# Split weights of the first MLP at another offset within their SBUF slots

## The chip, the cores and the metric

The kernel runs on one core of one Trainium2 chip. The metric is the device time of one execution in microseconds. Three runs of the kernel before gave 1238.68, 1238.93 and 1238.98 us, median 1238.93.

## What is computed

Three float32 stages follow one another; the weights of both MLPs come as 64-bit floats:

```python
# attention: 4 batches x 12 heads, 448 rows, head size 64
q_n, k_n = rmsnorm(q, g_q), rmsnorm(k, g_k)
x = softmax(q_n @ k_n.T / sqrt(64)) @ v            # -> 4 x 448 x 768
# first MLP, with layer norm and residual
xn = layernorm(x) * g_ln
y = x + relu(xn @ w_ch1) @ w_ch2                   # 768 -> 3072 -> 768
# gated MLP
h = relu(y @ w_in); u, v = h[..., :512], h[..., 512:]
v_s = einsum('ts,bsd->btd', w_spatial, layernorm(v)) + b_spatial
out = (u * v_s) @ w_out
```

## The kernel before, in words

Attention goes first, then the first MLP, then the gated MLP, one after the other on TensorE, with the seams overlapped. In the two MLPs every float32 operand is split in two float32r parts, a high part (a rounded copy) and a low part (the rest), and each product is three matmuls: high by high, high by low, low by high (the table `THREE`). The first number of a pair picks the part of the stationary operand, the second that of the moving one.

The first MLP works in units of 128 hidden columns, 24 units in all. For a unit u and a batch b, `h_pe` (L703) makes the hidden block: 6 slices of the 768 inputs by 3 products are 18 matmuls, with a 128x128 block of w_ch1 as the stationary operand and the normalized input `xn` (128 x 448) as the moving one. `h_act` and `h_dve` (L713, L718) take it out of PSUM as the split tile `h`. `o_pe` (L726) multiplies it by w_ch2: 6 output blocks by 3 products, again 18 matmuls with a stationary 128x128 block of weights. So there are 24 x 4 x 36 = 3456 matmuls, each 128x128 by 128x448, and all of them load their stationary operand from a `ws` tile.

A `ws` tile holds one unit's block of one weight matrix in both parts, 2 x 768 float32r values in each partition. It is made in `plan_parts`: ScalarE copies the converted weights `wc` into the high part (`hi`, through the helper at L101), GpSimd subtracts to get the low part (`lo`, L178). The conversion from 64-bit numbers (L91 to L95) stands ahead of it on ScalarE and VectorE. There are five slots for `ws` tiles: two in the pool `w0s`, which during attention also holds the normalized keys and queries (`kq`), and three in the pool `w1s`, which opens with the first MLP. The order of all instructions on every engine is written out by a planner (`arrange`) from estimated times and due numbers; it knows nothing of addresses.

In the gated MLP the same scheme of three products is used, with other tiles: `gv` (L797; moving `winv` 128x512, stationary the split `ys`, 112 columns), `gu` (L860; moving `ys` 128x448, stationary `winu`, 128 columns), `gs` (L881; moving `wsp_s` 112x448, stationary `gvs`, 128 columns), `gp` (L928; moving `wout` 128x384, stationary `gg`, 128 columns). `ys` lies in the buffer that held the `xn` of batch 0.

Where the tiles lie, from the built program: the first byte in the partition, and in brackets what is left after division by 256. All steps inside these tiles from slice to slice are multiples of 256 bytes, except in `ys` as a stationary operand, where the four column blocks c of 112 stand 448 bytes apart.

| tile | before | after |
|---|---|---|
| `ws`, pool `w0s` | 174048, 180192 (224) | 173728, 180128 (160) |
| `ws`, pool `w1s` | 103392, 109536, 115680 (224) | 102304, 108704, 115104 (160) |
| `kq`, in the slots of `w0s` | 174048, 180192 (224) | 173536, 179936 (224) |
| `xn`, batches 0 to 3 | 17120, 38624, 121824, 143328 (224) | 17120, 38624, 121312, 142816 (224) |
| `h` | 92640, 96224, 99808 (224) | 91360, 94944, 98528 (224) |
| `wc` | 89568, 170976 (224) | 88288, 170464 (224) |
| `ys` moving (`gu`) | 17120 (224) | the same |
| `ys` stationary (`gv`), c = 0, 1, 2, 3 | (224), (160), (96), (32) | the same |
| `winu`, stationary (`gu`) | 103072 (160) | the same |
| `winv`, moving (`gv`) | 60128 (224) | the same |
| `wsp_s` moving, `gvs` stationary (`gs`) | 88736 (160), 38624 (224) | the same |
| `wout` moving, `gg` stationary (`gp`) | 159200 (224), 200672 (224) | the same |

Of the kernel before, what the change touches and what calls it, by code (L numbers as in the profile page):

```python
# [10 lines left out]
F32R = mybir.dt.float32r  # L11
# [23 lines left out]
def f32(ap):  # L35
    return ap.bitcast(F32)
# [3 lines left out]
def attention_mlp_gated(ctx, tc, q, k, v, g_q, g_k, g_ln, w1, w2, w_in, w_sp, b_sp, w_out, out):  # L40
    nc = tc.nc
    B, H, S, D = q.shape
    DM, FF = w1.shape
    DG = w_out.shape[0]
    P = 128
# [54 lines left out]
    def act_copy(d, s):  # L100
        nc.scalar.activation(d, s, AF.Copy)  # L101
# [6 lines left out]
    wpools = {"raw": [], "c": [], "s": []}  # L108
    wsp, converted, pieces = {}, {}, []
# [56 lines left out]
    def plan_parts(i, n, since=()):  # L166
        kind, src, u = pieces[i]
        pl, c = converted[i], f"wc{i}"

        def hi():  # L170
            m = n_split[0] % 5
            n_split[0] += 1
            t = wsp[kind, u] = wpools["s"][int(m > 1)].tile([P, 2, DM], F32R, tag="ws", name=f"ws{i}")
            act_copy(t[:, 0], pl["c"])

        def lo():
            t = wsp[kind, u]
            nc.gpsimd.tensor_tensor(t[:, 1], pl["c"], f32(t[:, 0]), op=ALU.subtract)  # L178

        if kind == "gate":  # L180
            dma(n, src.shape[1] / 2, lambda: nc.sync.dma_start(u, pl["c"]), r=[c])
        else:
            op(n, "ACT", 0.73, hi, r=[c, *since], w=[f"{kind}_{u}"], new="ws")
            op(n, "POOL", 1.76, lo, r=[c], w=[f"{kind}_{u}"])
# [23 lines left out]
    def op(n, eng, us, fn, r=(), w=(), new=None, mode=None):  # L208

        ops.append((n, eng, us, fn, tuple(r), tuple(w), new, mode))  # L210

    def dma(n, kb, fn, **kw):

        op(n, "SP", max(0.6, kb / 360), fn, **kw)
# [757 lines left out]
    with tc.manual_schedule():  # L972
# [148 lines left out]
        n, i = 49, len(conv_at) + 3  # L1121
# [155 lines left out]
```

## Time and profile before

| | |
|---|---|
| median of three runs | 1238.93 us |
| profiled execution: its own time | 1238.33 us |
| profiled execution: span | 1236.3 us |
| TensorE busy | 1208.0 us, 98% of the span |
| VectorE, ScalarE, GpSimd busy | 796.3, 451.1, 325.3 us |
| matmuls of L703 and L726 | 1728 and 1728, 365.7 and 366.1 us busy |

The busy time of a group is the time in which at least one of its instructions ran; matmuls overlap, so that a single one is recorded with 365 ns while the next one starts well before that is over. What a matmul costs in a dense stretch is read from starts: the timeline merges like instructions into one row with the start of the first and their count, so the start of the next row less this start, divided by the count, is the cost of each.

### The profile page before, as it was taken

The numbers are of one execution on the slowest core, as the hardware profiler recorded it, in microseconds if no ns is written. First come the engines' busy times: TensorE is split into PE (matmuls) and PEld (weight loads), VectorE is DVE, ScalarE is ACT, GpSimd is POOL, SyncE is SP. The second block draws the span as 40 slices with busy tenths as digits, with TensorE's granted clock in tenths as the row PEclk, the third lists the DMA queues.
The fourth block names the chain that finished last, engine by engine and source line by source line (L and its number), as shares of the span: only waits on it lengthen the run. The fifth ranks groups of instructions, "written<-read, shape, count | busy, mean of one in ns | idle before, by whom it ended". The sixth has DMA issues, their size and how long they took to land.

```text
span 1236.3 us, 16695 instructions
## 1 busy us (share of the span) xinstructions
PE 1208.0 (98%) x6528; PEld 1021.6 (83%) x6528; DVE 796.3 (64%) x1436; ACT 451.1 (36%) x910; POOL 325.3 (26%) x266
## 2 busy tenths in 40 slices
PE   3999999999999999999999999999999999999998
PEld 1655656656999999999999999999999988889898
DVE  6889998976988656474747484755535577342240
ACT  2888888987432212131312121221202122123112
POOL 5764767524121102020202111010201115312120
PEclk9999999999999999999999999999999999999999
DMA  4213122111214232231313141502100053111103
GB/s 104 76 53 76 53 54 75 49 49 34 77 69 137 69 102 71 83 110 44 111 43 119 50 155 44 153 26 77 52 26 26 26 211 109 40 45 51 39 1 90
DMA packets 50861, 89.00 MB, mean 72 GB/s; under 512 B 3952, under 2 KB 39152, under 8 KB 50016
## 3 DMA queue, kind: packets, MB, share of 16 engines
q1 hardware_dynamic: 50352, 83.82, 22.1%
q10 hardware_dynamic: 432, 4.13, 0.8%
q8 instruction: 51, 0.84, 0.3%
q14 instruction: 26, 0.21, 0.1%
HBM read 73.58 MB, written 14.35 MB: 71 GB/s over the span
## 4 chain that ended last, share of the span: by engine, by line
PE 87%; DVE 9%; DMA 2%; POOL 1%; ACT 1%; issue 0%; SPq 0%; DVEq 0%
PE ph L703 28%; PE pm L726 28%; PE s L473 5%; PE gp L928 5%; PE po L523 4%; PE t L506 4%; PE gv L797 4%; PE gu L860 3%; PE gs L881 3%; DVE nmx L479 2%; DMA y_dram<-y 1%; PE pk L450 1%; DMA wout_r<-wout_dram 1%; DVE rt L80 1%; PE pq L450 1%; PE pxT L578 1%
## 5 line engine op out<-in xcount | busy, mean ns | idle before, releaser
L726 PE MATMUL pm<-h,ws 128*128 128x448 f32 x1728 | 366.1, 365 | 0.0
L703 PE MATMUL ph<-xn,ws 128*128 128x448 f32 x1728 | 365.7, 365 | 0.0
L726 PEld LDWEIGHTS pm<-h,ws 128*128 128x128 f32 x1728 | 324.3, 188 | 26.4 <-issue 0.7
L703 PEld LDWEIGHTS ph<-xn,ws 128*128 128x128 f32 x1728 | 324.4, 188 | 25.8 <-DVE y L734 0.2
L178 POOL TENSOR_TENSOR ws<-wc,ws 128x768 fp32r<-128x768 f32 x48 | 95.9, 1997 | 583.7 <-ACT ws L101 571.5
L734 DVE TENSOR_TENSOR y<-pm,y 128x448 f32<-128x448 f32 x318 | 176.1, 613 | 78.7 <-PE pm L726 78.7
L713 ACT ACTIVATE h<-ph 128x448 fp32r<-128x448 f32 x96 | 51.8, 540 | 276.5 <-PE ph L703 269.2
L718 DVE SCALAR_TENSOR_TENSOR h<-ph,h 128x448 fp32r<-128x448 f32 x96 | 59.6, 621 | 131.8 <-ACT h L713 130.2
L483 ACT ACTIVATE P<-s,nmx 112x448 f32<-112x448 f32 x192 | 119.2, 635 | 30.4 <-DVE nmx L479 30.1
L479 DVE TENSOR_REDUCE nmx<-s 112x2 f32<-112x896 f32 x96 | 101.1, 1080 | 18.7 <-PE s L473 18.2
L91 ACT ACTIVATE wc<-wr 128x768 f32<-128x768 f32 (+1 forms) x64 | 55.1, 862 | 136.6 <-POOL ws L178 45.2
L473 PE MATMUL s<-kT,qT 64*112 64x448 f32 x384 | 88.2, 580 | 0.6 <-ACT qT L459 0.6
L506 PE MATMUL t<-ident,P 112*112 112x112 f32 x768 | 85.4, 260 | 1.6 <-ACT P L483 1.1
L101 ACT ACTIVATE ws<-wc 128x768 fp32r<-128x768 f32 x48 | 40.6, 846 | 115.5 <-PE ph L703 99.2
L506 PEld LDWEIGHTS t<-ident,P 112*112 112x112 f32 x768 | 76.0, 133 | 4.8 <-ACT P L483 3.8
L523 PE MATMUL po<-PT,vr 112*64 112x448 f32 x384 | 77.5, 545 | 0.0
L95 DVE SCALAR_TENSOR_TENSOR wc<-wr,wc 128x768 uint32<-128x768 uint32 (+1 forms) x64 | 69.1, 1079 | 1.1
L94 DVE SCALAR_TENSOR_TENSOR wc<-wr,wc 128x768 int32<-128x768 int32 (+1 forms) x64 | 67.6, 1056 | 1.6
L92 DVE TENSOR_SCALAR wc<-wc 128x768 f32<-128x768 f32 (+1 forms) x64 | 37.4, 584 | 47.0 <-ACT wc L91 46.9
L797 PE MATMUL gv<-winv,ys 128*112 128x512 f32 x288 | 67.3, 393 | 0.0
L473 PEld LDWEIGHTS s<-kT,qT 64*112 64x112 f32 x384 | 31.4, 178 | 41.6 <-issue 23.4
L523 PEld LDWEIGHTS po<-PT,vr 112*64 112x64 f32 x384 | 25.4, 136 | 48.5 <-issue 38.4
(167 smaller groups left out, 1270.1 us busy)
## 6 DMA issues: line engine op xcount, KB each, us to landing
wr<-in_moe_w_ch_dram SPq DMA_DIRECT2D x48, 768.0 KB, 4.4
wr<-in_moe_w_in_dram SPq DMA_DIRECT2D x12, 512.0 KB, 3.8
vr<-in_v_dram SPq DMA_DIRECT2D x24, 224.0 KB, 2.7
kr<-in_k_dram SPq DMA_DIRECT2D x11, 448.0 KB, 3.9
qr<-in_q_dram SPq DMA_DIRECT2D x11, 448.0 KB, 4.8
y_dram<-y ACTq DMA_DIRECT2D x3, 1344.0 KB, 9.0
yl<-y_dram SPq DMA_DIRECT2D x3, 1344.0 KB, 6.2
win_dram<-wc SPq DMA_DIRECT2D x12, 256.0 KB, 5.1
```

The source lines that it names most:

```text
L94: lambda: v.scalar_tensor_tensor(ci, hi, -0x40000000, ci, op0=ALU.bitwise_and, op1=ALU.bitwise_or),
L95: lambda: v.scalar_tensor_tensor(cu, lo.bitcast(U32), 29, cu, op0=ALU.logical_shift_right, op1=ALU.bitwise_or),
L178: nc.gpsimd.tensor_tensor(t[:, 1], pl["c"], f32(t[:, 0]), op=ALU.subtract)
L473: nc.tensor.matmul(p[:CP, j, :S], pr["qT"][rows, c * CP : (c + 1) * CP], pr["kT"][rows], start=True, stop=True)
L479: nc.vector.tensor_reduce(t, pr["s", c][:CP, :, :S], axis=AX.X, op=ALU.max, negate=True)
L483: nc.scalar.activation(t, pr["s", c][:CP, j, :S], AF.Exp, bias=pr["m", c][:, j : j + 1], scale=1.0, accum_out=pr["sum"][:, j, c : c + 1],)
L506: nc.tensor.transpose(p[:CP, e, c * CP : (c + 1) * CP], pr["P", j, c][:, kc * CP : (kc + 1) * CP], ident[:CP, :CP])
L523: nc.tensor.matmul(pr["po"][j * D : (j + 1) * D, :S], raw["v", i][:, j, kc, :], pr["PT", kc // 2, j][:, kc % 2], start=(kc == 0), stop=(kc ...
L703: nc.tensor.matmul(hid[u, b][0][:, :S], s1[:, a, kk, :], xn[b][:, c, kk, :], start=(kk == 0 and m == 0), stop=(kk == NK - 1 and m == 2),)
L726: nc.tensor.matmul(po[:, :S], s2[:, a, m * P : (m + 1) * P], hs[:, c, :], start=(first and e == 0), stop=(last and e == 2),)
L734: nc.vector.tensor_tensor(y[b][:, m, :], po[:, :S], y[b][:, m, :], op=ALU.add)
L797: nc.tensor.matmul(pv[:CP, :], ys[b][:, a, kk, c * CP : (c + 1) * CP], W["v", kk][:, e], start=(kk == 0 and m == 0), stop=(kk == NK - 1 an ...
```

## The change

The slot of a `ws` tile is 64 float32 values (256 bytes) longer, and the split weights begin 48 values (192 bytes) into it. Every stationary address of L703 and L726, and every write of L101 and L178 to `ws`, moves with them; nothing else reads these tiles. The pools that are allocated behind these slots move down by 512 or 1280 bytes, whole multiples of 256. Instructions, their operands' shapes and their order on every engine are the same as before.

```diff
@@ -170,7 +170,9 @@
         def hi():
             m = n_split[0] % 5
             n_split[0] += 1
-            t = wsp[kind, u] = wpools["s"][int(m > 1)].tile([P, 2, DM], F32R, tag="ws", name=f"ws{i}")
+            t = wsp[kind, u] = wpools["s"][int(m > 1)].tile([P, 2 * DM + 64], F32R, tag="ws", name=f"ws{i}")[
+                :, 48 : 48 + 2 * DM
+            ].rearrange("p (a f) -> p a f", a=2)
             act_copy(t[:, 0], pl["c"])
```

## Rows read from the trace of the kernel before

**Rows 1.** Page: busy time by engine, TensorE and clock over 40 slices.

```profile
PE 1208.0 (98%) x6528; PEld 1021.6 (83%) x6528; DVE 796.3 (64%) x1436; ACT 451.1 (36%) x910; POOL 325.3 (26%) x266
...
PE   3999999999999999999999999999999999999998
...
PEclk9999999999999999999999999999999999999999
```

**Rows 2.** Page: the chain that ended last, by engine and by line.

```profile
PE 87%; DVE 9%; DMA 2%; POOL 1%; ACT 1%; issue 0%; SPq 0%; DVEq 0%
PE ph L703 28%; PE pm L726 28%; PE s L473 5%; PE gp L928 5%; PE po L523 4%; PE t L506 4%; PE gv L797 4%; PE gu L860 3%; PE gs L881 3%; DVE nmx L479 2%; DMA y_dram<-y 1%; PE pk L450 1%; DMA wout_r<-wout_dram 1%; DVE rt L80 1%; PE pq L450 1%; PE pxT L578 1%
```

**Rows 3.** Waits of TensorE over the span: total us, times, longest.

```profile
PE pk L450 <- DVE kq L412: 13.4, 1, 13.4
PE pk L450 <- POOL kq L412: 6.4, 1, 6.4
PE t L506 <- ACT P L483: 1.1, 4, 0.6
PE psp L1197 <- DVE wsp_s L1203: 0.8, 1, 0.8
PE gs L881 <- POOL gvs L838: 0.7, 1, 0.7
```

**Rows 4.** Windows: busy us (instructions) of each engine, clock, DMA.

```profile
core 0: us, PE busy (x) PEld busy (x) DVE busy (x) ACT busy (x) POOL busy (x), PEclk, DMA share, GB/s
...
328.00:1014.00 686.00, 686.00 (x3387) 634.54 (x3386) 428.17 (x673) 147.33 (x221) 96.96 (x50) 1.00 0.24 79
...
1038.00:1236.00 198.00, 193.57 (x977) 174.99 (x975) 71.06 (x139) 45.64 (x88) 39.13 (x28) 1.00 0.14 42
```

**Rows 5.** Timeline of TensorE, 600 to 632 us, first MLP: start, us, what.

```profile
602.41 3.81 PE L703 MATMUL ph<-xn,ws 128*128 128x448 f32 x18
606.06 3.81 PE L726 MATMUL pm<-h,ws 128*128 128x448 f32 x18
...
631.60 0.57 PE L703 MATMUL ph<-xn,ws 128*128 128x448 f32 x2
```

**Rows 6.** Timeline of TensorE, 1103 to 1164 us, gated MLP.

```profile
1109.11 14.56 PE L860 MATMUL gu<-ys,winu 128*128 128x448 f32 x72
1123.51 29.31 PE L928 MATMUL gp<-wout,gg 128*128 128x384 f32 x168
1152.66 9.87 PE L881 MATMUL gs<-wsp_s,gvs 112*128 112x448 f32 x48
1162.36 1.80 PE L797 MATMUL gv<-winv,ys 128*112 128x512 f32 x7
```

**Rows 7.** The same, 1172 to 1216 us.

```profile
1178.91 14.56 PE L860 MATMUL gu<-ys,winu 128*128 128x448 f32 x72
1193.31 9.87 PE L881 MATMUL gs<-wsp_s,gvs 112*128 112x448 f32 x48
```

**Rows 8.** Timeline of weight loads, batch 2, blocks c = 0 to 3 (four windows).

```profile
1092.36 4.08 PEld L797 LDWEIGHTS gv<-winv,ys 128*112 128x112 f32 x18
1096.49 4.08 PEld L797 LDWEIGHTS gv<-winv,ys 128*112 128x112 f32 x18
1100.63 4.11 PEld L797 LDWEIGHTS gv<-winv,ys 128*112 128x112 f32 x18
1104.81 4.03 PEld L797 LDWEIGHTS gv<-winv,ys 128*112 128x112 f32 x18
```

**Rows 9.** The same for batch 1, block c = 3.

```profile
1064.06 4.11 PEld L797 LDWEIGHTS gv<-winv,ys 128*112 128x112 f32 x18
```

**Rows 10.** Timeline, 312 to 330 us: the first units.

```profile
311.84 0.77 PE L726 MATMUL pm<-h,ws 128*128 128x448 f32 x3
312.45 0.93 PE L578 MATMUL pxT<-ident,x 112*128 112x112 f32 x8
313.33 7.57 PE L703 MATMUL ph<-xn,ws 128*128 128x448 f32 x36
```

**Rows 11.** Timeline of all engines, 354 to 364 us: the third unit's weights.

```profile
356.71 0.85 ACT L101 ACTIVATE ws<-wc 128x768 fp32r<-128x768 f32 x1 [1.55 <-DVE wc L95]
...
357.63 2.22 POOL L178 TENSOR_TENSOR ws<-wc,ws 128x768 fp32r<-128x768 f32 x1 [30.93 <-ACT ws L101]
...
361.44 2.62 PEld L703 LDWEIGHTS ph<-xn,ws 128*128 128x128 f32 x13
```

**Rows 12.** Groups by line and form, 328 to 1014 us: makers of `ws`, a load.

```profile
L178 POOL TENSOR_TENSOR ws<-wc,ws 128x768 fp32r<-128x768 f32 x44 | 88.3, 2008 | 537.4 <-ACT ws L101 525.1 <-issue 12.3
...
L101 ACT ACTIVATE ws<-wc 128x768 fp32r<-128x768 f32 x44 | 37.2, 845 | 111.9 <-PE ph L703 99.2 <-PE pm L726 6.2 <-DVE wc L95 5.9
...
L797 PEld LDWEIGHTS gv<-winv,ys 128*112 128x112 f32 x30 | 5.2, 174 | 1.6
```

## Prediction

> **What bounds the kernel now.** I read the page first, then the waits of TensorE, the windows by stage, and last the timeline of TensorE alone, since the question is what one matmul costs. The page shows TensorE busy for 98% of the span, with the clock granted in full in all 40 slices [rows 1]. In the chain that ended last TensorE has 87%, and the two lines of the first MLP, L703 and L726, have 28% each: 56% of the span hangs on the 3456 matmuls whose stationary operand is the tile that moves [rows 2]. The waits of TensorE are two long ones for `kq` at the start and then a microsecond here and there; no line of the first MLP stands among the longest [rows 3]. Between 328 and 1014 us TensorE is busy in all of the 686.0 us, while VectorE has 428.2, ScalarE 147.3 and GpSimd 97.0 [rows 4]. There the end is set by nothing but the pace of the matmuls, and any change of that pace reaches the end in full.
>
> A busy TensorE is not one at its best pace, so the pace itself has to be looked at. From 602.41 to 631.60 us there are eight groups of 18 matmuls: 29.19 us over 144 is 202.7 ns each [rows 5]. At 2.4 GHz, the upper level of the clock, 448 columns are 186.7 ns, so 16.0 ns come on top. In the gated MLP the line `gu` has the same shape, 128x128 by 128x448, and the same order of three products, and its moving operand lies in the very buffer that holds `xn` of batch 0 here. It takes 1123.51 - 1109.11 = 14.40 us for 72 matmuls, 200.0 ns each [rows 6], and the same 14.40 us one batch later [rows 7]: 13.3 ns on top of its columns. `gp` with 384 columns takes 29.15 us for 168, 173.5 ns, which is 160.0 + 13.5 [rows 6]. The fourth column block of `gv` in batch 2, with 512 columns, has 17 intervals and one load of 174 ns in 4.03 us: 226.8 ns, or 213.3 + 13.5 [rows 8, 12]. So three shapes agree on a floor of columns plus 13.3 to 13.5 ns, and the matmuls of the first MLP stand 2.7 ns above it.
>
> What raises a matmul above the floor is seen best inside `gv`, where the moving operand, the shape and the order are the same in the four blocks of a batch, and only the stationary operand begins elsewhere: at 224, 160, 96 and 32 bytes past a multiple of 256. The starts give 4.13 us, 4.14 us and 4.18 us for 18 in the first three, 229.4, 230.0 and 232.2 ns, against 226.8 in the fourth [rows 8]. The place of the stationary operand is thus worth up to 5.4 ns per matmul. `gs`, with its moving operand at 160 and its stationary one at 224, has 9.70 us for 48, 202.1 ns [rows 6], also above the 200.0 of its column count.
>
> **The change part by part.** It adds no instruction, no wait and no transfer, and moves none past another on any queue, SP's and GpSimd's among them. What it moves is the stationary address of 3456 matmuls, from 224 to 160 past a multiple of 256, while their moving operands stay at 224. That pair, 160 and 224, at 448 columns and 128 stationary columns, is the pair of `gu`. So the row that stands nearest to the changed matmul is 200.0 ns, and I take it.
>
> The sum: the first 18 of L703 and the first 18 of L726 lie among the last attention work, before the row at 313.33 us [rows 10], and I leave them out; 3456 - 36 = 3420 matmuls gain 202.7 - 200.0 = 2.7 ns each, unrounded 2.71, together 9.3 us. The unknown price of the pair is bounded from both sides by the rows of `gv`: best, at the floor, as in the fourth block, -9.3 us; worst, 5.4 ns above it, as in the third, (5.4 - 2.7) x 3420 = +9.2 us. I take the lower end because `gu` shares shape, order and moving buffer with the changed lines, and no `gv` row does.
>
> One rule of the Trainium skill speaks against this. First the rows: the same moving buffer and the same shape run at 202.7 ns with one stationary tile and at 200.0 ns with another [rows 5, 6], and four column blocks of one stationary tile differ by up to 5.4 ns [rows 8]. The Trainium skill, "TensorE: Matmul & The Clock Gate", Part 2 (step by step, on LDWEIGHTS), says that TensorE has two independent read ports, so that loading the next weights takes nothing from the running matmul; by that the place of the weights would not matter and the time would stay at 1238.9 us. The rows of this trace do not bear it out to the last nanosecond, which is where this change lives; so the rule keeps a chance as the first rival, no more.
>
> The writers of `ws` move too. The copy takes 845 ns on ScalarE and the subtraction 2008 ns on GpSimd [rows 12]; no row has either at the new offset, so their price is anything from a gain to a doubling. It is hidden: GpSimd is busy for 97.0 of 686.0 us [rows 4], and the tightest hand-over is the third unit's, whose low part is done at 357.63 + 2.22 = 359.85 us while its first load starts at 361.44, 1.59 us later [rows 11]. A faster TensorE comes there earlier by 2.7/202.7 of the 48.1 us since 313.33, 0.64 us; 0.95 us of cover is left. If the subtraction took more than 0.95 us longer, this one unit would wait for the difference, once, under 1.3 us even when it doubled. I take zero.
>
> With TensorE 1.3% faster in this stretch, VectorE's share goes from 428.2/686.0, 62%, to 63%, and the transfers, at a mean share of 0.24 [rows 4], have room; nothing is late next.
>
> The pools behind the slots move by whole multiples of 256, and the gated MLP's tiles do not move: zero for both, in time per instruction. One thing can flip there: the fourth block of `gv` ran at 226.8 ns in batch 2 and, with the same addresses, at (4.11 - 0.174)/17 = 231.5 ns in batch 1 [rows 8, 9]. So the pace also hangs on how a stretch is entered. Four such blocks x 18 x 4.7 ns are 0.34 us; two may flip either way, +-0.2 us.
>
> The sum against the profiled execution: its span is 1236.3 us and its own time 1238.33, so 2.0 us lie around the span; 1238.33 - 9.3 = 1229.0. That execution is 0.6 us under the median of the three runs, 1238.93, so on the scale of the median the forecast is 1238.93 - 9.3 = 1229.7 us.
>
> **The rivals.** The first: nothing happens, 1238.9 us. Either the 2.7 ns come from something other than the place of the weights (the PSUM buffers, or the distance of 3072 bytes between the two parts, which in `winu` is 2048), or the shift keeps whatever matters. For it: `gp` has both operands at 224 and stands at its floor, 173.5 ns [rows 6], so 224 with 224 is not bad at every column count. Against it: `gv` changes its pace with nothing but the column block [rows 8]. Chance 12%.
>
> The second ends on the other side: the new pair makes matmul and weight load meet more often, not less. In `gv` block 1, at 160 with 224 as after the change, is 230.0 ns, 0.6 ns slower than block 0 at 224 with 224 [rows 8]. If the order of `gv` holds, L703 and L726 go from 2.7 ns above the floor to about 2.7 x 3.2/2.6 = 3.3, which is +2.1 us, 1241.0; at the third block's 5.4 ns it is 1238.9 + 9.2 = 1248.1. It decides from a pace above 202.7 ns on. Against it stands that `gv` has 512 columns and 112 stationary ones, and `gu`, with the right numbers of both, is at the floor in each row that I have [rows 6, 7]. Chance 15%.
>
> The third: the floor is reached in part of the stretch alone. For it: the fourth block of `gv` has two paces at one address [rows 8, 9]; and of the five new slots only two (173728 and 108704) agree with `winu` in their rest after division by 512 too, the other three being 256 further. If two in five units gain, it is 0.4 x 9.3 = 3.7 us, 1235.2; if half the time is gained, 1234.3. Against it: the moving slices of 1792 bytes step by 256 from one to the next modulo 512, in `gu` and in L703 alike, so that either relation has occurred in `gu`, and its whole 72 still come out at 200.0 [rows 6]. Chance 9%.
>
> **How the numbers follow.** The forecast, near the floor throughout, has 64%, and its own range is 1228.8 to 1230.8: +-0.3 us for the spread of the runs, the flips in `gv`, up to 0.7 us for the third unit's cover. The range that holds the time 8 times in 10 starts at 1228.7 and goes up through the third rival and the first to 1239.5, which leaves out the second rival, 15%, and a little below. No change within 0.2% (2.5 us, about what a measurement of this kernel can tell from none) is 1236.5 to 1241.4: the first rival's 12%, and one part in three of the second, 5%, together 17%. Slower is the rest of the second, 10%. Faster is 64% + 9%, 73%.
>
> **What would show it.** In the changed kernel's timeline the groups of 18 should start 3.60 us apart in place of 3.65, in L703 and L726 alike, whatever the batch or the slot; `gu`, `gp`, `gs` and `gv` should keep their paces; the waits of TensorE should show no `ws`. If only the units of two slots quicken, the third rival was right; if the groups stand 3.65 us apart, the first; 3.66 or more, the second. The forecast fails at the step from `gu` to L703 if anything but the place of the weights sets their 2.7 ns.

## The result, and the profile after

Five runs of the changed kernel have the median 1229.24 us (1227.83 to 1229.59), five of the kernel before beside them 1238.93 us. The ratio is 0.9918 with a 95% interval of 0.9907 to 0.9930: 9.7 us less, and forecast were 9.3. The profiled execution took 1229.24 us with a span of 1227.5, 8.8 us less than the span before. All line numbers behind L174 are two higher in the changed kernel.

The page of the changed kernel, busy time and the chain by engine and line:

```profile
PE 1198.8 (98%) x6528; PEld 1020.5 (83%) x6528; DVE 794.9 (65%) x1436; ACT 451.3 (37%) x910; POOL 325.1 (26%) x266
...
PE 89%; DVE 7%; DMA 2%; ACT 1%; issue 0%; POOL 0%; SPq 0%; DVEq 0%
PE ph L705 28%; PE pm L728 28%; PE s L475 5%; PE gp L930 5%; PE gu L862 5%; PE gv L799 4%; PE po L525 4%; PE t L508 4%; PE gs L883 3%; DVE nmx L481 2%; DMA win_ru<-win_dram 1%; PE pk L452 1%; PE pq L452 1%; PE pxT L580 1%; DVE PT L518 1%; PE px L559 1%
```

Against [rows 1, 2] the number of instructions is the same and TensorE is busy for 9.2 us less, while the other engines keep their busy times within 1.5 us. In the chain L705 and L728 keep their 28% each, and TensorE has 89% in place of 87%. The reader should notice how little the page tells: a share of 98% stays 98% while the work inside it gets faster.

The pace, in the timeline of TensorE in the first MLP of the changed kernel:

```profile
603.22 3.76 PE L728 MATMUL pm<-h,ws 128*128 128x448 f32 x18
606.82 3.76 PE L705 MATMUL ph<-xn,ws 128*128 128x448 f32 x18
...
628.41 3.76 PE L705 MATMUL ph<-xn,ws 128*128 128x448 f32 x18
```

Seven groups of 18 take 628.41 - 603.22 = 25.19 us, 199.9 ns each, where [rows 5] had 202.7. The groups start 3.60 us apart. In the gated MLP of the changed kernel nothing moved:

```profile
1100.26 14.56 PE L862 MATMUL gu<-ys,winu 128*128 128x448 f32 x72
1114.66 29.31 PE L930 MATMUL gp<-wout,gg 128*128 128x384 f32 x168
1143.81 9.87 PE L883 MATMUL gs<-wsp_s,gvs 112*128 112x448 f32 x48
1153.52 2.72 PE L799 MATMUL gv<-winv,ys 128*112 128x512 f32 x11
```

`gu` takes 14.40 us for its 72, `gp` 29.15 for 168, `gs` 9.71 for 48, to 0.01 us what [rows 6] show.

The whole span can be cut at two starts, the first pair of hidden blocks in the dense stretch ([rows 10], 313.33 us) and the first `gv`. Timeline of TensorE, the kernel before:

```profile
1007.33 2.92 PE L797 MATMUL gv<-winv,ys 128*112 128x512 f32 x12
```

and the two places in the kernel after (two windows):

```profile
314.30 7.47 PE L705 MATMUL ph<-xn,ws 128*128 128x448 f32 x36
...
999.21 4.07 PE L799 MATMUL gv<-winv,ys 128*112 128x512 f32 x17
```

The stretch took 694.00 us before and takes 684.91 after: -9.09 us. The attention ahead of it ends 0.97 us later in this execution, the rest behind it is 0.68 us shorter (228.97 and 228.29); the sum is -8.80, the difference of the spans. The waits of TensorE in the kernel after show where most of the 0.97 comes from:

```profile
PE pk L452 <- DVE kq L414: 14.1, 1, 14.1
PE pk L452 <- POOL kq L414: 6.4, 1, 6.4
PE psp L1199 <- DVE g L815: 1.1, 1, 1.1
```

The wait for the first keys is 14.1 us in place of the 13.4 of [rows 3], 0.7 of the 0.97. The wait of `gs` for GpSimd, 0.7 us in [rows 3], is gone, while that of `psp` (small transposes in the gated MLP) is 1.1 us in place of 0.8: together 0.4 of the 0.68. These are seams outside the first MLP, and no `ws` stands among the longest waits.

The hand-over that was tightest, in the timeline of all engines of the kernel after:

```profile
358.10 2.23 POOL L180 TENSOR_TENSOR ws<-wc,ws 128x768 fp32r<-128x768 f32 x1 [30.37 <-ACT ws L101]
...
358.42 3.76 PE L728 MATMUL pm<-h,ws 128*128 128x448 f32 x18
...
361.82 3.58 PEld L705 LDWEIGHTS ph<-xn,ws 128*128 128x128 f32 x18
...
362.01 3.76 PE L705 MATMUL ph<-xn,ws 128*128 128x448 f32 x18
```

The subtraction takes 2.23 us, as before (2.22), and 1.49 us of cover are left of the 1.59 in [rows 11]. The prediction left only 0.95: counted from the start of the dense stretch, the load is 0.59 us earlier than before, but the subtraction is 0.50 us earlier too.

### The profile page after: what moved, and what is told of

It reads as the page before. It is cut to its first block, busy times and chain, and to the rows that moved or that the text cites. A ratio compares the mean times of both kernels' runs of the same rounds, so it can differ in the third digit from the quotient of the medians.

```text
span 1227.5 us, 16696 instructions
## 1 busy us (share of the span) xinstructions
PE 1198.8 (98%) x6528; PEld 1020.5 (83%) x6528; DVE 794.9 (65%) x1436; ACT 451.3 (37%) x910; POOL 325.1 (26%) x266
## 4 chain that ended last, share of the span: by engine, by line
PE 89%; DVE 7%; DMA 2%; ACT 1%; issue 0%; POOL 0%; SPq 0%; DVEq 0%
PE ph L705 28%; PE pm L728 28%; PE s L475 5%; PE gp L930 5%; PE gu L862 5%; PE gv L799 4%; PE po L525 4%; PE t L508 4%; PE gs L883 3%; DVE nmx L481 2%; DMA win_ru<-win_dram 1%; PE pk L452 1%; PE pq L452 1%; PE pxT L580 1%; DVE PT L518 1%; PE px L559 1%
## 5 line engine op out<-in xcount | busy, mean ns | idle before, releaser
L728 PE MATMUL pm<-h,ws 128*128 128x448 f32 x1728 | 361.6, 362 | 0.0
L705 PE MATMUL ph<-xn,ws 128*128 128x448 f32 x1728 | 361.1, 362 | 0.0
L728 PEld LDWEIGHTS pm<-h,ws 128*128 128x128 f32 x1728 | 323.7, 187 | 22.4 <-issue 0.7
L705 PEld LDWEIGHTS ph<-xn,ws 128*128 128x128 f32 x1728 | 323.8, 187 | 21.8 <-DVE y L736 0.2
L101 ACT ACTIVATE ws<-wc 128x768 fp32r<-128x768 f32 x48 | 40.6, 845 | 113.1 <-PE ph L705 97.2
```

The lines of the kernel that those rows point to most:

```text
L705: nc.tensor.matmul(hid[u, b][0][:, :S], s1[:, a, kk, :], xn[b][:, c, kk, :], start=(kk == 0 and m == 0), stop=(kk == NK - 1 and m == 2),)
L728: nc.tensor.matmul(po[:, :S], s2[:, a, m * P : (m + 1) * P], hs[:, c, :], start=(first and e == 0), stop=(last and e == 2),)
```

## Experiments

The theory from the prediction, called A: the pace of these matmuls depends on where the stationary operand begins against the moving one, modulo 256 bytes. In what follows "distance" is the start of the stationary operand less that of the moving one, modulo 256: it was 0 before and is 192 after. Where A has to be told from A2 it is called A1. The rivals: the longer slots or the moved pools (B); the stationary operand's place alone (A2); a pace that is locked in at the start of a stretch (H).

**1. The longer slots alone.**

```diff
-...tile([P, 2, DM], F32R, tag="ws", name=f"ws{i}")
+...tile([P, 2 * DM + 64], F32R, tag="ws", name=f"ws{i}")[:, 0 : 2 * DM].rearrange("p (a f) -> p a f", a=2)
```

> The slots are 256 bytes longer as in the change, but the split weights begin at the slot's start, so the stationary operands of L703 and L726 stay 224 bytes past a multiple of 256, and the pools behind them move as in the change. Theory A (the place of the stationary operand against the moving one sets the pace): the pace stays at 202.7 ns, about 1238.9 us. Theory B (the longer slots, or the moved pools behind them, made the gain): 200.1 ns, about 1229.3 us.

Measured: 1238.69 us, ratio to before 0.9998 (0.9989 to 1.0007). Timeline of TensorE:

```profile
602.45 3.81 PE L705 MATMUL ph<-xn,ws 128*128 128x448 f32 x18
...
613.39 2.80 PE L728 MATMUL pm<-h,ws 128*128 128x448 f32 x13
```

Three groups in 10.94 us: 202.6 ns. The longer slots and all that they push down do nothing; B falls.

**2. Weights and moving operands both 192 bytes in.**

```diff
+weights as in the change
-xn[b] = xn_pool.tile([P, 2, NK, S], F32R, ...)
+xn[b] = xn_pool.tile([P, 2 * NK * S + 64], F32R, ...)[:, 48 : 48 + 2 * NK * S].rearrange("p (a k s) -> p a k s", a=2, k=NK)
-hs = pl.tile([P, 2, S], F32R, ...)
+hs = pl.tile([P, 2 * S + 64], F32R, ...)[:, 48 : 48 + 2 * S].rearrange("p (a s) -> p a s", a=2)
```

> The weights lie 192 bytes in as in the change, and the moving operands xn and h lie 192 bytes into longer buffers too; both now begin 160 bytes past a multiple of 256. Theory A1 (the distance between stationary and moving operand decides): back at 202.7 ns, about 1238.9 us. Theory A2 (the place of the stationary operand by itself decides): 200.1 ns, about 1229.3 us.

Measured: 1238.85 us, ratio 1.0019 (0.9994 to 1.0044). Timeline of TensorE:

```profile
602.60 3.81 PE L707 MATMUL ph<-xn,ws 128*128 128x448 f32 x18
...
613.55 2.80 PE L732 MATMUL pm<-h,ws 128*128 128x448 f32 x13
```

10.95 us for 54, 202.8 ns. With the weights at exactly the residue of the change, but the moving operands moved along, the gain is gone. Two of the twelve executions behind the median took 1252.56 and 1253.21 us, with TensorE's clock granted in full; the other ten lie between 1238.26 and 1239.42, and the kernel before, at the same distance 0, never took more than 1240.6 in the 23 executions beside them. Spread over the 3420 matmuls, the 14.0 us that they are longer would make 206.8 ns of each 202.7, an estimate from the times alone: neither was profiled, so whether the pace was another at the same addresses stays open.

**3. The moving operands alone, 64 bytes on.** The same edit of `xn` and `h` with 16 in place of 48, the weights as before.

> The weights stay where they were before (224); xn and h begin 64 bytes later (32 past a multiple of 256), so the stationary operand lies 64 bytes behind the moving one modulo 256, as in the change. A1: 200.1 ns, about 1229.3 us. A2: 202.7 ns, about 1238.9 us.

Measured: 1229.03 us, ratio 0.9919 (0.9907 to 0.9932). Timeline of TensorE:

```profile
602.41 3.76 PE L730 MATMUL pm<-h,ws 128*128 128x448 f32 x18
...
613.21 2.96 PE L705 MATMUL ph<-xn,ws 128*128 128x448 f32 x14
```

10.80 us for 54, 200.0 ns, with `ws` untouched. Experiments 2 and 3 together show that in the profiled executions the distance decides and not the place of either operand: A2 falls, A stands, and the change could as well have been made on the other side.

**4. The same in the gated MLP.**

```diff
+weights as in the change
-t = W[key, kk] = pl.tile([P, 2, DG], F32R, ...)
+t = W[key, kk] = pl.tile([P, 2 * DG + 64 * e], F32R, ...)[:, 16 * e : 16 * e + 2 * DG].rearrange("p (a f) -> p a f", a=2)
-W["sp"] = cw.tile([CP, 2, NCH, S], F32R, name="wsp_s")
+W["sp"] = cw.tile([CP, 2 * NCH * S + 64], F32R, name="wsp_s")[:, 32 : 32 + 2 * NCH * S].rearrange("p (a c s) -> p a c s", a=2, c=NCH)
```

> The change, and in the gated MLP the moving operands are moved: winv 64 bytes on (gv: stationary less moving is 192, 128, 64, 0 for the column blocks c = 0 to 3 in place of 0, 192, 128, 64), wsp_s 128 bytes on (gs: 192 in place of 64). A1: gs falls from 202.3 to 200.0 ns, 0.4 us in all; gv's paces go round by one block: about 230.0, 232, 226.7 or 231.6, 229.4 to 231 ns for c = 0 to 3, no change in its sum beyond 0.3 us; time 1229.2 less 0.4. A2: gs and gv keep their paces, 1229.2 us.

Measured: 1228.59 us (1228.10 to 1229.19), ratio to before 0.9916 (0.9903 to 0.9928). Timeline of TensorE:

```profile
1143.18 9.77 PE L883 MATMUL gs<-wsp_s,gvs 112*128 112x448 f32 x48
1152.79 16.77 PE L799 MATMUL gv<-winv,ys 128*112 128x512 f32 x72
1169.40 14.56 PE L862 MATMUL gu<-ys,winu 128*128 128x448 f32 x72
1183.80 9.78 PE L883 MATMUL gs<-wsp_s,gvs 112*128 112x448 f32 x48
1193.41 21.85 PE L930 MATMUL gp<-wout,gg 128*128 128x384 f32 x125
```

`gs` falls to 9.61 us for 48, 200.2 ns, in both batches shown (1143.18 to 1152.79, 1183.80 to 1193.41), from 202.1 to 202.3: the theory told in advance what a product of another stage would do when its moving operand is shifted. The paces of `gv`, from the starts of the matmuls inside a block, go round as expected in three of four blocks of batches 1 to 3: 230.3, 231.9, 231.7 and 228.7 ns for c = 0 to 3 (distances 192, 128, 64, 0); before they were 230.1 to 230.4 at 192, 231.6 to 231.9 at 128, 231.7 or 226.6 at 64, 231.1 to 231.4 at 0. The last block was expected at 229.4 to 231. It is the fastest of the versions run by its median, but 0.65 us under the change is less than these runs can tell apart; only the trace shows the 0.4 us.

**5 and 6. A map of the distance.** Each pair of units gets an offset of its own, so one run holds twelve distances (one execution each, 1238.47 and 1239.08 us):

```diff
+o = (0, 8, 16, 24, 32, 40, 48, 56, 52, 44, 36, 60)[u // 2]     # second run: (4, 12, 20, 28, 50, 46, 58, 62, 54, 42, 48, 16)
+...tile([P, 2 * DM + 64], F32R, tag="ws", ...)[:, o : o + 2 * DM].rearrange("p (a f) -> p a f", a=2)
```

> Each pair of units of the first MLP has its own offset in the longer slots, so that stationary less moving is 0, 32, 64, 96, 128, 160, 192, 224, 208, 176, 144, 240 bytes modulo 256 for the pairs 0 to 11. Theory A (the distance decides, at each moment, whatever came before): 202.7 ns at 0 and 200.0 at 192 within this one run, the step at the first matmuls of a pair; by the order of gv, 128 is the worst, up to 205, and 64 either 200 or 205. Theory H (one locks in at the start of a stretch and keeps it): the pairs carry on the pace of the pair before, so 192 after 160 could stay slow. In the gated MLP wsp_s lies 192 bytes on (gs at distance 128: 203 to 205 ns in place of 202.3 by A) and wout 64 bytes on (gp at 192: 173.4 stays if 384 columns are too few to meet; 2 to 5 ns more if the distance works there too).

> The same with distances 16, 48, 80, 112, 200, 184, 232, 248, 216, 168, 192, 64 for the pairs 0 to 11. Theory A: 192 again 200.0, now after 168, and 64 with the pace that it has in the run with 64 after 32; its neighbours 184 and 200 within 0.3 ns of 200.0 if the good place has a width, else near 202.7. Theory H: 192 and 64 come out otherwise than in the other run. In the gated MLP winv lies 224 bytes on (gv at 32, 224, 160, 96 for c = 0 to 3) and wsp_s too (gs at 96): paces between those of their neighbours, 229 to 232 and 202 to 203, if they go smoothly with the distance.

Measured, as the mean from start to start over the 287 or 288 matmuls of each distance (144 for 0 and 16, which come first, behind the last attention work):

| distance | 0 | 16 | 32 | 48 | 64 | 80 | 96 | 112 | 128 | 144 | 160 | 168 |
|---|---|---|---|---|---|---|---|---|---|---|---|---|
| ns | 202.6 | 206.6 | 204.4 | 202.2 | 202.2 | 203.3 | 200.4 | 204.0 | 204.0 | 202.2 | 205.3 | 206.6 |

| distance | 176 | 184 | 192 | 200 | 208 | 216 | 224 | 232 | 240 | 248 |
|---|---|---|---|---|---|---|---|---|---|---|
| ns | 203.3 | 204.5 | 200.0 | 200.1 | 204.4 | 203.4 | 204.6 | 202.2 | 200.0 | 200.0 |

Inside the groups of 18 alone, without the steps from one group to the next, the means differ by up to 0.2 ns; the expectations of the later experiments quote such means. The map is not smooth: 8 or 16 bytes apart lie 206.6 (168), 203.3 (176), 204.5 (184), 200.0 (192), 200.1 (200) and 204.4 (208). Nothing is below 200.0. The two distances that stand in both runs, 64 and 192, come out alike, 202.2 and 202.2, 200.0 and 200.0. How a new distance is entered shows in the timeline of TensorE at the step from 160 to 192 (first run; the output line runs one batch behind the hidden line, so L729 still has 160 at 658.15 us):

```profile
647.16 3.86 PE L706 MATMUL ph<-xn,ws 128*128 128x448 f32 x18
650.86 3.85 PE L729 MATMUL pm<-h,ws 128*128 128x448 f32 x18
654.55 3.76 PE L706 MATMUL ph<-xn,ws 128*128 128x448 f32 x18
658.15 3.86 PE L729 MATMUL pm<-h,ws 128*128 128x448 f32 x18
661.85 3.77 PE L706 MATMUL ph<-xn,ws 128*128 128x448 f32 x18
665.45 3.76 PE L729 MATMUL pm<-h,ws 128*128 128x448 f32 x18
```

and from 168 to 192 (second run):

```profile
885.39 3.88 PE L729 MATMUL pm<-h,ws 128*128 128x448 f32 x18
889.10 3.77 PE L706 MATMUL ph<-xn,ws 128*128 128x448 f32 x18
892.71 3.88 PE L729 MATMUL pm<-h,ws 128*128 128x448 f32 x18
896.42 3.76 PE L706 MATMUL ph<-xn,ws 128*128 128x448 f32 x18
900.02 3.76 PE L729 MATMUL pm<-h,ws 128*128 128x448 f32 x18
```

3.70, 3.69, 3.60, 3.70, 3.60 us in the first, 3.71, 3.61, 3.71, 3.60 in the second: group by group the pace follows the distance of that group. H, a pace kept from the stretch before, falls for the first MLP. A neighbour can still count where a lone group stands between groups of another distance, as the last output group at 96 does between hidden groups at 128 (first run):

```profile
540.33 3.87 PE L729 MATMUL pm<-h,ws 128*128 128x448 f32 x18
544.04 3.84 PE L706 MATMUL ph<-xn,ws 128*128 128x448 f32 x18
```

It takes 3.71 us, 206.1 ns, where the groups at 96 ahead of it settled at 200.0; the last group at 224, between groups at 208, also takes 3.71 us. The guesses for 64 (200 or 205), for 128 as the worst and for a smooth course were wrong. At `gs` the distance 96 costs 200.1 to 200.7 ns and 128 costs 203.9 to 204.1 in three batches, as the map has it, but 206.5 in batch 1 (48 matmuls from 1082.67 us on, first run); `gp` at 192 keeps 173.3.

**7 and 8. Which two operands meet?** The records show the load of the next weights beside the running matmul (in the kernel after, the first load of a group starts at 361.82 us and its matmul at 362.01, while the group before still runs), so theory N pairs the next stationary operand with this matmul's moving one; theory S pairs the two operands of one matmul. High and low parts with offsets of their own set them apart:

```diff
+# run 7: low part of ws 32 bytes later (160, 192), low part of xn and h 32 bytes later (224, 0)
+# run 8: low part of ws 48 bytes later (160, 208), low part of xn and h 48 bytes earlier (224, 176)
```

> High and low parts get offsets of their own: weights high at 160, low at 192, moving high at 224, low at 0 (past multiples of 256). Each product of three is (high, high), (high, low), (low, high), stationary first. Theory N (what counts is the stationary operand of the NEXT matmul, loaded while this one's moving operand streams): the pairs are next high with this high twice, and next low with this low: 192, 192, 192, all at the floor, 200.0 ns, about 1229.3 us. Theory S (stationary and moving operand of the SAME matmul): 192, 160 and 224, of which the maps gave 200.0, 205.3 and 204.5: a mean near 203.3, about 1241 us. In the gated MLP winv lies 240 bytes on: gv at 16, 208, 144, 80 for c = 0 to 3, no theory of its own, for the map at 512 columns.

> The reverse: weights high at 160, low at 208, moving high at 224, low at 176. Theory S: the pairs of the same matmul are 192, 240 and 240, each at the floor in the maps, so 200.0 ns and about 1229.3 us. Theory N: next high with this high twice, 192, and next low with this low, 32, where the maps gave 204.3: a mean near 201.4, about 1234 us, and not 200.0. In the gated MLP winv lies 208 bytes on: gv at 48, 240, 176, 112 for c = 0 to 3, for the map.

Measured: 1241.26 us for the first, 1229.13 us for the second, one run each beside 1238.84 of the kernel before. Timeline of TensorE of run 7, and behind it of run 8:

```profile
604.16 3.82 PE L708 MATMUL ph<-xn,ws 128*128 128x448 f32 x18
...
629.73 2.60 PE L732 MATMUL pm<-h,ws 128*128 128x448 f32 x12
```

```profile
602.17 3.76 PE L730 MATMUL pm<-h,ws 128*128 128x448 f32 x18
...
616.57 3.76 PE L730 MATMUL pm<-h,ws 128*128 128x448 f32 x18
```

25.57 us for 126, 202.9 ns, and 14.40 us for 72, 200.0 ns. S said 203.3 and 200.0, N 200.0 and 201.4: N falls in both.

**9. The order of the three products.** In the old order S cannot be told from a theory N2, by which a moving operand meets the weights two matmuls ahead (or one behind): the set of pairs is the same. With the offsets of run 7:

```diff
+MLP3 = ((0, 0), (1, 0), (0, 1))    # in h_pe and o_pe in place of THREE = ((0, 0), (0, 1), (1, 0))
```

> The offsets of the run in which high and low parts had distances 192, 160 and 224 in the same matmul (203.0 ns), with the three products of the first MLP in the order (high, high), (low, high), (high, low), stationary first. Theory S (operands of the same matmul) has the same three distances 192, 224, 160 in another order: about 203.0 ns again, 1241 us. Theory N2 (this matmul's moving operand meets the weights of the matmul two ahead, or of the one behind): in the old order it could not be told from S; in the new one its pairs are high with high, high with high, low with low, 192 each: 200.0 ns, about 1229.2 us.

Measured: 1244.44 us in one run beside 1238.75 of the kernel before; timeline of TensorE:

```profile
605.23 3.84 PE L709 MATMUL ph<-xn,ws 128*128 128x448 f32 x18
...
612.59 3.64 PE L709 MATMUL ph<-xn,ws 128*128 128x448 f32 x17
```

7.36 us for 36, 204.4 ns. N2 falls; S has the side right, but not the size: 204.4 where the same three distances in the other order gave 202.9. So a mixture of distances is not the mean of its parts, and the pair inside one matmul is not all that counts: the order is worth 1.5 ns here, which no theory of these explains.

**10. 168 bytes in place of 192.** `[:, 42 : 42 + 2 * DM]` in place of `[:, 48 : 48 + 2 * DM]`, nothing else.

> The change with the split weights 168 bytes into the longer slots in place of 192, everything else the same: distance 168, where the fine map gave 206.7 ns. Theory A: 3420 matmuls x (206.7 - 202.7) = 13.7 us more than the kernel before, 1252.5 us, slower by 1.1%. Theory B (any offset off the multiple of 256 helps): about 1229 us.

Measured: 1252.64 us (1251.66 to 1252.97), ratio to before 1.0112 (1.0095 to 1.0129). Timeline of TensorE:

```profile
603.92 3.88 PE L728 MATMUL pm<-h,ws 128*128 128x448 f32 x18
...
615.08 1.19 PE L705 MATMUL ph<-xn,ws 128*128 128x448 f32 x5
```

11.16 us for 54, 206.7 ns, and the whole kernel comes out within 0.2 us of 1252.5. The map carries over to the time of the kernel, on the slow side too.

## Why the prediction was right

The step that carried it, from `gu` to L703 and L726, held: the same distance, shape and moving buffer gave the same pace, 200.0 ns forecast and 199.9 measured, in all units. The size held too: 9.27 us forecast for the dense stretch, 9.09 measured there. The other 0.6 of the 9.7 between the medians lie outside this stretch or differ from execution to execution; no run shows which.

The bounds at zero also held. The writers of `ws` keep their durations, the third unit's cover stays, `gp`, `gu` and `gs` keep their paces, and in the profiled execution none of the `gv` blocks flipped.

Of the rivals, the first (no effect of the place of the weights) is refuted by the result with experiment 1, where the same slots without the offset give no gain. With it falls what the prediction drew from the Trainium skill, "TensorE: Matmul & The Clock Gate", Part 2, that the place of the weights would not matter: the measured spread by place is 6.7 ns of 200. What the Trainium skill itself states there, that loading the next weights takes nothing from the running matmul, is neither shown nor refuted by these runs: the pairing with the next weights fell in experiments 7 and 8. That the two streams meet in memory is a reading, not a measurement. The third rival (two of five slots) is refuted by the profile after: groups of all slots start 3.60 us apart, and a further 256 bytes make no difference.

The second rival was reasoned wrongly, though it did no harm. Its order of the `gv` blocks came from the starts of weight loads [rows 8], and the first load of a stretch starts while the stage before still runs. The starts of the matmuls in the same batch, a window for each block, have another order (timeline of TensorE, the kernel before):

```profile
1092.56 4.32 PE L797 MATMUL gv<-winv,ys 128*112 128x512 f32 x18
1096.72 4.30 PE L797 MATMUL gv<-winv,ys 128*112 128x512 f32 x18
1100.87 4.33 PE L797 MATMUL gv<-winv,ys 128*112 128x512 f32 x18
1105.03 4.24 PE L797 MATMUL gv<-winv,ys 128*112 128x512 f32 x18
```

The first three blocks take 4.16, 4.15 and 4.16 us (231.1, 230.3 and 231.4 ns from the unrounded starts): block 1, the pair of the change, is not slower than block 0 but 0.8 ns faster (in batch 0, at the start of the stage, it is 0.7 ns slower), and the spread to the fourth block is 4.8 ns in place of 5.4. The rival also took the order of the `gv` paces for a guide to the first MLP. At the distance 192, where 448 columns run at 200.0 ns, `gv` with 512 columns and 112 stationary ones stands 3.5 ns above its floor; the map does not carry over from one shape to the other, and it was right to give `gu`, the row of the same shape, the greater weight. The rival's price was real, and the bound on it too low: an offset of 168 bytes costs 13.9 us beside the kernel before, where the prediction took 9.2 us for the worst.

The own range of the forecast had +-0.3 us for the spread of the runs; the five runs lie between 1227.83 and 1229.59. What makes that spread is not shown.

## What to carry to other kernels

Where TensorE is busy without a gap, read the pace from start to start for each line and compare lines of one shape: a floor that one line reaches and another misses by a per cent, with nothing waiting, can be a sign of where the operands lie. Moving either operand's buffer by a few tens of bytes cost 256 bytes a slot here and was worth a per cent either way, so the distance has to be mapped and not guessed, best with many offsets in one run, and for each shape by itself. A change that shifts allocations for another reason can move the time by such a per cent as well, and should be read with this in mind.

## What the runs showed of the hardware that was not expected

- With 448 moving columns the pace runs from 200.0 to 206.7 ns with the distance, in no smooth order, and is the same at 96 (but for its first groups and its last), 192, 200, 240 and 248. The distance alone does not always fix it: one lone group at 96 had 206.1 ns, one batch of `gs` at 128 had 206.5 where the others had 204, and the two long executions of experiment 2 are unexplained.
- With 384 columns (`gp`) both distances tried, 0 and 192, give 173.3 to 173.5 ns.
- With 512 columns and 112 stationary ones (`gv`) the sixteen distances in steps of 16 gave 226.6 to 233.6 ns in batches 1 to 3, and a few had several paces at one distance: at 64, 226.6 or 231.6; at 0, from 228.7 to 233.6; at 160, 226.8 in these batches and 233.4 in batch 0. What picks the pace there stays open.
- Of the pairings tried, only that of the two operands of one matmul fits the side of experiments 7, 8 and 9, although the records show its weights being loaded beside the matmul before it. How the two come to meet is open; no run here shows it.
- The offset also changes the subtraction on GpSimd that writes `ws`. By tile, the kernel after and, behind it, experiment 10 (minimum/median/maximum in ns):

```profile
L180 POOL TENSOR_TENSOR ws<-wc,ws x48: 1834/1867/2447, 272.6 to 943.2; 128x768 fp32r<-128x768 f32 x48
L180 POOL TENSOR_TENSOR ws<-wc,ws x48: 1541/1552/2336, 271.1 to 962.6; 128x768 fp32r<-128x768 f32 x48
```

  In the second map, too, the subtractions of the offsets 168, 184, 200, 216, 232 and 248 bytes took mostly about 1.55 us, and those of offsets that are multiples of 16 bytes 1.8 or more. It is hidden here, since GpSimd is busy for 97.0 of 686.0 us [rows 4].
